# An induced-attention block and a rational mixture layer on one core: the odd unit's numerator ahead of the next mask, token sums from accumulated exponentials, and the second layer thirteen ticks behind with fifteen rooms

## The chip, the cores and the metric

The kernel runs on one core of a Trainium2 chip. The metric is the device time of one execution in microseconds (us). The engines are named as in the profile: PE (matmul; PEld are its weight loads), DVE (vector), ACT (scalar activation), POOL (GpSimd) and SP, which only issues DMAs. Each runs its own instructions in order and waits for the others by semaphores.

## The reference

There are 4 batches of 12480 tokens with 128 channels, and 32 inducing points. First the inducing points attend over the tokens, then the tokens attend over the 32 results. Each token then goes through two layers with 2048 hidden values, with a rational function between them:

```python
def mab(q, kv):
    s = scale * (q @ kv.transpose(0, 2, 1))
    s = s - s.max(-1, keepdims=True)
    a = np.exp(s)
    a /= a.sum(-1, keepdims=True) + 1e-09
    return a @ kv
h = mab(I, x)
attn_out = mab(x, h)
...
h = x @ w_in
h2 = h * h
h3 = h2 * h
P = a[0] + a[1] * h + a[2] * h2 + a[3] * h3
Q = 1.0 + np.abs(b[0]) * np.abs(h) + np.abs(b[1]) * h2
g = P / (Q + 1e-06)
return (g @ w_out).astype(np.float32)
```

## The kernel before

**Units and ticks.** A chunk is 480 tokens; a batch has 26 chunks. The hidden layer is cut into 8 parts of 256, so a chunk has 8 units and the whole run 832. One unit is a tile of 128 partitions x 2 x 480. `fast_ticks` (L777) writes out one loop over ticks t; in tick t it issues pieces of work for units of different age, and the order in which it issues them is the order on each engine (`InOrder`, L147, pins it; since all calls go through L157 there, the profile puts that line to nearly everything, and groups are told apart by their tiles).

**One unit's way.** `first` (L729) is the first layer into a PSUM tile `hp` (3 rooms). For an *even* unit DVE takes |h| into `u` (the **mask**, group `u<-hp`, L807); POOL makes the **opening** (|h| + k1, group `l<-u,all`, L813) into a tile of tag `l`; a tick later DVE makes the **even numerator** (`l<-hp,all,l`, L802), the last reader of `hp`. For an *odd* unit ACT takes **Abs** (`u<-hp,all`, L821) in its own tick, and DVE makes the **odd numerator** (`l<-u,all,hp`, L810) a tick later, also the last reader of `hp`. The two `u` of an even and an odd unit lie in one pair tile. ACT turns the pairs into the reciprocal of the denominator: four **Ln** (`u<-u`, L816) and four **Sigmoid** (`u<-u,all`, L818) in eight ticks, with a table load at each turn from one to the other. The variable `turn` (L788) counts the eight ticks. Exponentials of the attention go in at turn 4, ahead of the first Sigmoid.

In an odd tick the even unit that is 11 ticks old gets its last **product** on DVE (`l<-l,all,u`, L799: all operands in SBUF), and the odd unit that is 10 ticks old gets the same in two steps on POOL (`last_on_pool`, L827: `u<-l,all`, which writes into the `u` that the product reads, then `l<-u`). `second` (L744) multiplies the unit that is 12 ticks old with `w_out` into the PSUM tile `po` and adds up the 8 units of a chunk there. The `l` tile of a unit lives from its opening or numerator to this matmul; there are 14 rooms of `l`.

So DVE's order over a pair of ticks is: mask, odd numerator, other work, product, even numerator, other work. POOL's is: opening, `u<-l,all`, `l<-u`, with other work behind the opening or behind `l<-u`.

**The other work.** `side` (L680) closes each tick. It moves a finished `po` to SBUF by an **oT** copy on DVE and issues the store (`fetch`, L762), and then hands out steps of two generators as far as the spare time of each engine allows (`SPARE`, L175): `ahead` (L633) prepares the next batch (`pass1`: scores and their maxima; `pooled`: sums of tokens weighted by exponentials; `piece`, `linear`: the first layer's weights times the attention's result), and `attend` (L658) scores the tokens of the current batch a few chunks ahead. A unit with part 0 of its chunk is `late` (L790): its second layer is issued at the end of the tick, behind `side`.

**Token sums.** `pass1` leaves scores in the tile `e`; `exp_rows` (L380) exponentiates them in place. `pooled` (L403) turns them into tiles `eT` (2 rooms) and multiplies them with token rows, `x_rows` (L282), tiles of 4 x 129 columns, of which the last is filled with ones by POOL; so column 128 of the result is the sum of the exponentials. H, the normalised result, is turned and repeated into `HT` (2 rooms), which `piece`, `linear` and the scoring of the tokens read. `scored` is the last batch whose scoring is issued.

**The start.** `before` (L858) runs `pass1` and `pooled` for batch 0 and loads and converts the weights, with the first layer's PSUM rooms lent out; the raw weights lie in rooms of `l`.

## Time and profile before

| | us |
|---|---|
| median of 3 runs | 2594.55 |
| the runs | 2594.13 to 2599.68 |
| the profiled execution | 2594.75 |
| its span, from the first to the last instruction | 2592.9 |

The profile page gives the busy time of each engine, the chain of work that ended last, and groups of like instructions with count, busy time, mean duration and the idle time ahead of them with its releaser. In a group `out<-in`, names are those of tiles. The waits list how long an engine waited for which releaser; the timeline lists instructions of an engine in order of time, where a bracket gives the idle time ahead of one. The mean granted TensorE clock of the run was 0.966. The start takes about 115 us; the first oT copy is at 156.3 us, the last at 2587.7 us, and there are 104, one for each chunk. `pass1`, `pooled` and `piece` of later batches end at about 1700 us; after that `attend` alone runs beside the units.

### The profile page before, as it was taken

Reading aid. Unit: us, or ns where it says so; the run is one execution under the profiler, and the core shown is the slowest. Engines: PE = TensorE matmul, PEld = TensorE weight load, DVE = VectorE, ACT = ScalarE, POOL = GpSimd, SP = SyncE. Lnnn points to the kernel's source line nnn. Section 1 sums busy time; section 2 is a strip of 40 time slices with the busy share of each in tenths; the row PEclk is TensorE's granted clock in tenths of the full one; section 3 lists DMA queues with packets and bytes.
Section 4 is the critical chain, followed back from the end, with each engine's and each line's share of the span. In section 5 each row is a group of like instructions: output and inputs, shape, how many; then the busy total and the mean of one; then the engine's idle time right before and its main releaser. Section 6 shows DMA issues by size and latency. Waiting matters only on the chain.

```text
span 2592.9 us, 24006 instructions
## 1 busy us (share of the span) xinstructions
PE 2249.2 (87%) x7508; PEld 1233.8 (48%) x7508; DVE 2210.1 (85%) x2318; ACT 2244.9 (87%) x1590; POOL 2011.4 (78%) x1420
## 2 busy tenths in 40 slices
PE   7798888999899789989988898888888888888887
PEld 4544444555454355544544465444435434434333
DVE  6578778899899889899898888988889888888886
ACT  1488889989889999888899998899999999999996
POOL 2267767888787788888687887887888887888887
PEclk9699989999999999999999999999999999999999
DMA  7222201211222012112321131011101001000000
GB/s 251 73 62 78 73 27 52 71 50 31 70 83 80 19 31 76 50 48 63 92 55 48 35 88 38 16 42 31 46 27 50 27 20 38 20 22 24 17 17 17
DMA packets 117357, 133.68 MB, mean 52 GB/s; under 512 B 13544, under 2 KB 115816, under 8 KB 117224
## 3 DMA queue, kind: packets, MB, share of 16 engines
q1 hardware_dynamic: 117224, 132.06, 17.6%
q8 instruction: 64, 1.05, 0.2%
q14 instruction: 69, 0.57, 0.1%
HBM read 80.89 MB, written 25.56 MB: 41 GB/s over the span
## 4 chain that ended last, share of the span: by engine, by line
DVE 32%; PE 22%; ACT 19%; POOL 18%; issue 6%; DMA 1%; SPq 1%; DVEq 0%; POOLq 0%; ACTq 0%
DVE l L157 21%; ACT u L157 13%; POOL l L157 13%; PE po L157 13%; DVE u L157 7%; ACT L157 4%; POOL u L157 4%; PE hp L157 3%; PE ph L157 2%; PE pd L157 2%; DVE oT L157 1%; POOL a L157 1%; SPq L157 1%; DVE asm L157 1%; DMA x<-x_t 1%
## 5 line engine op out<-in xcount | busy, mean ns | idle before, releaser
L157 PE MATMUL po<-l,w_out 128*128 128x480 f32 x3328 | 1545.8, 592 | 188.4 <-POOL l L157 183.6
L157 PEld LDWEIGHTS po<-l,w_out 128*128 128x128 f32 x3328 | 607.3, 194 | 773.0 <-issue 419.7
L157 POOL TENSOR_TENSOR l<-u 128x960 f32<-128x960 f32 x416 | 932.2, 2241 | 34.7
L157 ACT ACTIVATE u<-u 128x1920 f32<-128x1920 f32 x416 | 739.8, 1799 | 193.2 <-DVE l L157 143.0
L157 PE MATMUL hp<-at,st 128*128 128x480 f32 x1664 | 742.7, 529 | 98.3 <-DVE l L157 91.1
L157 ACT ACTIVATE u<-u,all 128x1920 f32<-128x1920 f32 x416 | 766.1, 1887 | 1.2
L157 POOL TENSOR_SCALAR u<-l,all 128x960 f32<-128x960 f32 x416 | 445.5, 1071 | 392.8 <-DVE l L157 363.4
L157 DVE SCALAR_TENSOR_TENSOR l<-l,all,u 128x960 f32<-128x960 f32 x416 | 597.8, 1437 | 105.7 <-ACT u L157 105.3
L157 DVE SCALAR_TENSOR_TENSOR l<-hp,all,l 128x960 f32<-128x960 f32 x416 | 503.5, 1210 | 121.8 <-POOL l L157 114.0
L157 POOL TENSOR_SCALAR l<-u,all 128x960 f32<-128x960 f32 x416 | 555.6, 1336 | 64.7 <-DVE u L157 63.7
L157 DVE TENSOR_SCALAR u<-hp 128x960 int32<-128x960 int32 x416 | 477.0, 1147 | 75.6 <-PE hp L157 74.3
L157 PEld LDWEIGHTS hp<-at,st 128*128 128x128 f32 x1664 | 312.6, 193 | 431.3 <-issue 325.3
L157 DVE SCALAR_TENSOR_TENSOR l<-u,all,hp 128x960 f32<-128x960 f32 x416 | 500.3, 1203 | 0.3 <-ACT u L157 0.3
L157 ACT ACTIVATE u<-hp,all 128x960 f32<-128x960 f32 x416 | 434.7, 1045 | 36.4 <-PE hp L157 36.3
L157 ACT ACT_TABLE_LOAD x234 | 300.2, 1283 | 4.9 <-PEq L942 0.7
L157 PE MATMUL ph<-x,eT 120*32 120x129 f32 x832 | 105.8, 280 | 9.0 <-DMA x<-x_t 6.3
L157 PEld LDWEIGHTS pd<-HT,xTb 128*120 128x120 f32 x832 | 103.3, 198 | 9.7 <-DMA xTb<-x_c 4.3
L157 PE MATMUL pd<-HT,xTb 128*120 128x32 f32 x832 | 100.5, 277 | 5.2 <-DMA xTb<-x_c 4.1
L157 PEld LDWEIGHTS ph<-x,eT 120*32 120x32 f32 x832 | 88.9, 112 | 28.0 <-issue 21.5
L157 DVE COPY oT<-po 128x480 f32<-128x480 f32 x104 | 67.3, 647 | 21.6 <-PE po L157 21.3
L157 PE MATMUL po<-at,st 128*128 128x480 f32 x104 | 80.7, 776 | 0.0
L157 PE MATMUL pc<-xTa,ind 128*128 128x480 f32 x156 | 72.2, 566 | 1.9 <-DMA xTa<-x_c 1.9
(84 smaller groups left out, 621.6 us busy)
## 6 DMA issues: line engine op xcount, KB each, us to landing
x<-x_t SPq DMA_DIRECT2D x104, 240.0 KB, 3.5
xTb<-x_c SPq DMA_DIRECT2D x104, 240.0 KB, 2.8
at<-hl SPq DMA_DIRECT2D x416, 60.0 KB, 2.0
out<-oT SPq DMA_DIRECT2D x104, 240.0 KB, 2.0
xTa<-x_c SPq DMA_DIRECT2D x78, 240.0 KB, 2.8
xTw<-x_c SPq DMA_DIRECT2D x5, 960.0 KB, 10.3
raw<-w_in SPq DMA_DIRECT2D x4, 480.0 KB, 14.2
raw<-w_out SPq DMA_DIRECT2D x5, 384.0 KB, 5.9
```

Of the source, the lines that this page charges most:

```text
L157: ins = call(*args, **kw)
```

## The change

- **Order on DVE.** In an even tick the odd numerator of the unit before is issued ahead of the mask.
- **Second layer.** `second` takes the unit that is 13 ticks old, `late` goes by that unit, the loop has one tick more, and `l` has 15 rooms. A late unit now falls in an odd tick, and the oT copy in an even one.
- **Token sums.** The exponentials' activation adds up its results by row (`accum_out`) into a tile `sums`; at the end DVE reduces it to one column and a matmul with `sum4` (four stacked unit matrices) adds the four row groups. The column of ones, its memsets on POOL and the 129th column of the sums are gone; a token-row tile is now contiguous.
- **Memory.** `eT` has one room (in the start it takes rooms of `l`), `HT` has one room, and its matmul waits until the batch before is scored; the table of constants has 88 columns.

```diff
@@ -47,7 +47,7 @@
 
     def __init__(self, nc, pool, moe_a, moe_b):
         self.nc, self.pool, self.n = nc, pool, 0
-        self.all = pool.tile([P, 128], F32, name="all")
+        self.all = pool.tile([P, 88], F32, name="all")
         ab = pool.tile([P, 6], F32, name="ab")
         nc.sync.dma_start(out=ab[:, 0:4], in_=moe_a.rearrange("(o n) -> o n", o=1).broadcast_to((P, 4)))
         nc.sync.dma_start(out=ab[:, 4:6], in_=moe_b.rearrange("(o n) -> o n", o=1).broadcast_to((P, 2)))
...
@@ -259,6 +259,10 @@
         self.ident4 = cp.tile([M, 4, M], F32, name="ident4")
         for j in range(4):
             nc.vector.tensor_copy(out=self.ident4[:, j], in_=self.ident[0:M, 0:M])
+        self.sum4 = cp.tile([P, M], F32, name="sum4")
+        nc.vector.tensor_copy(out=self.sum4, in_=self.ident[:, 0:M])
+        for j in range(1, 4):
+            nc.vector.tensor_tensor(out=self.sum4, in0=self.sum4, in1=self.ident[:, M * j:M * j + M], op=ALU.add)
         self.w_in = cp.tile([C, self.F], F32, name="w_in")
         self.w_out = cp.tile([P, self.NF, C], F32, name="w_out")
 
...
@@ -273,22 +277,21 @@
             dst = self.w_out[:, c].rearrange("p f d -> p (f d)")
             parts.append((self.w_out_d[P * c.start:P * c.stop, :].rearrange("(f p) d -> p f d", p=P), dst, C * (c.stop - c.start)))
         for n, (src, dst, width) in enumerate(parts):
-            tag, bufs = ("l", 14) if width > 2 * P else ("oT", 2)
+            tag, bufs = ("l", 15) if width > 2 * P else ("oT", 2)
             raw = self.mp.tile([P, width], mybir.dt.int64, tag=tag, name=f"raw{n}", bufs=bufs)
             self.nc.sync.dma_start(out=raw if len(src.shape) == 2 else raw.rearrange("p (f d) -> p f d", d=C), in_=src)
             yield raw, dst, width
 
 
     def x_rows(self, b, n):
-        t = self.ap.tile([TP, HB, C + 1], F32, tag="xa", name=f"x{b}_{n}", bufs=4)
-        self.nc.sync.dma_start(out=t[:, :, 0:C], in_=self.x_t[b, :, HB * n:HB * n + HB, :])
-        self.nc.gpsimd.memset(t[:, :, C:], 1.0)
+        t = self.ap.tile([TP, HB, C], F32, tag="xa", name=f"x{b}_{n}", bufs=4)
+        self.nc.sync.dma_start(out=t, in_=self.x_t[b, :, HB * n:HB * n + HB, :])
         self.issued["x", b, n] = self.tick
         return t
 
     def x_columns(self, b, n, kind):
         if kind == "a":
-            t = self.ap.tile([C, HB * (C + 1)], F32, tag="xa", name=f"xTa{b}_{n}", bufs=4)[:, 0:BT]
+            t = self.ap.tile([C, HB * C], F32, tag="xa", name=f"xTa{b}_{n}", bufs=4)[:, 0:BT]
         else:
             t = self.ap.tile([C, BT], F32, tag="xTb", name=f"xTb{b}_{n}", bufs=4)
         self.nc.sync.dma_start(out=t, in_=self.x_c[b, :, BT * n:BT * n + BT])
...
@@ -338,6 +341,8 @@
         e = ap.tile([P, self.NG, BT], F32, tag="e", name=f"e{b}")
         mxs = ap.tile([P, self.NG, 2], F32, tag="mxs", name=f"mxs{b}")
         nc.gpsimd.memset(mxs, -3.0e38)
+        self.sums[b] = ap.tile([P, self.NG], F32, tag="sums", name=f"sums{b}")
+        nc.gpsimd.memset(self.sums[b], 0.0)
         xs = self.wide_columns(b) if self.boot else self.cols.pop((b, "a"))
         for g in range(self.NG):
             nb = min(4, self.NB - 4 * g)
...
@@ -384,7 +389,7 @@
         rows = slice(0, M * min(4, self.NB - 4 * (g + n - 1)))
         if n == 2 and rows.stop < P:
             n, rows = 1, slice(0, P)
-        self.nc.scalar.activation(e[rows, g:g + n], e[rows, g:g + n], AF.Exp, bias=nmc[rows], scale=1.0 / math.sqrt(C))
+        self.nc.scalar.activation(e[rows, g:g + n], e[rows, g:g + n], AF.Exp, bias=nmc[rows], scale=1.0 / math.sqrt(C), accum_out=self.sums[b][rows, g:g + 1])
         self.e_done[b] = g + n
         if g + n < self.NG:
             if self.boot:
...
@@ -404,7 +409,7 @@
 
         nc, ap = self.nc, self.ap
         e = self.e[b]
-        acc = ap.tile([M, C + 1], F32, tag="acc", name=f"acc{b}")
+        acc = ap.tile([M, C], F32, tag="acc", name=f"acc{b}")
         xs = self.xs.pop(b)
 
         def turned(g):
...
@@ -414,7 +419,10 @@
                 if c == 0:
                     pt = self.misc(f"pt{b}_{g}").rearrange("p (c n) -> p c n", c=HB)
                 nc.tensor.transpose(out=pt[0:TP, c, rows], in_=e[rows, g, TP * c:TP * c + TP], identity=self.ident[rows, rows])
-            eT = ap.tile([TP, HB, P], F32, tag="eT", name=f"eT{b}_{g}", bufs=2)
+            if self.boot:
+                eT = self.mp.tile([TP, 2, BT], F32, tag="l", name=f"eT{b}_{g}", bufs=15).rearrange("p a n -> p (a n)")[:, 0:HB * P].rearrange("p (c n) -> p c n", n=P)
+            else:
+                eT = ap.tile([TP, HB, P], F32, tag="eT", name=f"eT{b}_{g}")
             yield from self.act(lambda: nc.scalar.activation(eT[:, :, rows], pt[0:TP, :, rows], AF.Identity, bias=0.0, scale=1.0))
             eTs.append(eT)
 
...
@@ -438,27 +446,34 @@
                     ph = self.misc(f"ph{b}_{g}")
                 if c == 0 and 0 < 4 * g + j < self.NB - 3:
                     xs.append(self.x_rows(b, 4 * g + j + 3))
-                nc.tensor.matmul(ph[0:M, 0:C + 1], eT[:, c, M * j:M * j + M], xs[4 * g + j][:, c, :], start=(k == 0), stop=(k == HB * nb - 1))
+                nc.tensor.matmul(ph[0:M, 0:C], eT[:, c, M * j:M * j + M], xs[4 * g + j][:, c, :], start=(k == 0), stop=(k == HB * nb - 1))
             yield "v", 0.2
             if g == 0:
-                nc.vector.tensor_copy(out=acc, in_=ph[0:M, 0:C + 1])
+                nc.vector.tensor_copy(out=acc, in_=ph[0:M, 0:C])
             else:
-                nc.vector.tensor_tensor(out=acc, in0=ph[0:M, 0:C + 1], in1=acc, op=ALU.add)
+                nc.vector.tensor_tensor(out=acc, in0=ph[0:M, 0:C], in1=acc, op=ALU.add)
             self.free()
+        yield "v", 0.1
+        es = ap.tile([P, 1], F32, tag="es", name=f"es{b}")
+        nc.vector.tensor_reduce(out=es, in_=self.sums[b], axis=mybir.AxisListType.X, op=ALU.add)
+        yield "pe", 0.2
+        pr = self.misc(f"prs{b}")
+        nc.tensor.matmul(pr[0:M, 0:1], self.sum4, es, start=True, stop=True)
         yield "v", 0.2
         rs = ap.tile([M, 1], F32, tag="rs", name=f"rs{b}")
-        nc.vector.tensor_scalar(out=rs, in0=acc[:, C:], scalar1=1e-9, scalar2=None, op0=ALU.add)
+        nc.vector.tensor_scalar(out=rs, in0=pr[0:M, 0:1], scalar1=1e-9, scalar2=None, op0=ALU.add)
+        self.free()
         nc.vector.reciprocal(out=rs, in_=rs)
         yield "v", 0.2
         H = ap.tile([M, C], F32, tag="H", name=f"H{b}")
-        nc.vector.tensor_scalar(out=H, in0=acc[:, 0:C], scalar1=rs, scalar2=None, op0=ALU.mult)
+        nc.vector.tensor_scalar(out=H, in0=acc, scalar1=rs, scalar2=None, op0=ALU.mult)
+        while own is None and b > 1 and self.scored < b - 1:
+            yield "wait", 0
         yield "pe", 0.3
         pt = self.misc(f"HT{b}")
         nc.tensor.matmul(pt[:, 0:4 * M], H, self.ident4.rearrange("p a m -> p (a m)"), start=True, stop=True)
         yield "v", 0.2
-        while own is None and self.scored < b - 2:
-            yield "wait", 0
-        HT = own if own is not None else ap.tile([C, 4 * M], F32, tag="HT", name=f"HT{b}", bufs=2)
+        HT = own if own is not None else ap.tile([C, 4 * M], F32, tag="HT", name=f"HT{b}")
         nc.vector.tensor_copy(out=HT, in_=pt[:, 0:4 * M])
         self.free()
         self.HT[b] = HT
...
@@ -783,15 +798,16 @@
         n = len(units)
         at = lambda t: units[t] if 0 <= t < n else None
         self.first(units[0])
-        for t in range(n + 13):
+        for t in range(n + 14):
             u, last, d = at(t), at(t - 1), at(t - 11)
             group, turn = divmod(t - 6, 8)
             w = at(8 * group + 2 * (turn % 4))
-            late = at(t - 12) and at(t - 12).key[2] == 0
+            done = at(t - 13)
+            late = done and done.key[2] == 0
             if late:
                 self.fetched = self.fetch()
-            if at(t - 12) and not late:
-                self.second(at(t - 12))
+            if done and not late:
+                self.second(done)
             if at(t + 1):
                 self.first(at(t + 1))
             if t % 2:
...
@@ -801,15 +817,15 @@
                 if last:
                     V.scalar_tensor_tensor(out=last.g, in0=last.h, scalar=p.k2, in1=last.g, op0=ALU.add, op1=ALU.mult)
             else:
+                if last:
+                    last.g = self.new(last, "l", 15)
+                    V.scalar_tensor_tensor(out=last.g, in0=last.u, scalar=p.k1, in1=last.h, op0=ALU.add, op1=ALU.mult)
                 if u:
                     u.pair = self.mp.tile([P, 2, 2, BT], F32, tag="u", name=f"u{u.i}", bufs=7)
                     u.u = u.pair[:, 0]
                     V.tensor_scalar(out=u.u.bitcast(I32), in0=u.h.bitcast(I32), scalar1=0x7FFFFFFF, scalar2=None, op0=ALU.bitwise_and)
-                if last:
-                    last.g = self.new(last, "l", 14)
-                    V.scalar_tensor_tensor(out=last.g, in0=last.u, scalar=p.k1, in1=last.h, op0=ALU.add, op1=ALU.mult)
                 if u:
-                    u.g = self.new(u, "l", 14)
+                    u.g = self.new(u, "l", 15)
                     G.tensor_scalar(out=u.g, in0=u.u, scalar1=1.0, scalar2=p.k1, op0=ALU.mult, op1=ALU.add)
             self.run_act(turn == 4)
             if w and turn < 4:
...
@@ -821,7 +837,7 @@
                 A.activation(u.u, u.h, AF.Abs, bias=p.back, scale=1.0)
             self.side(u or units[-1])
             if late:
-                self.second(at(t - 12))
+                self.second(done)
         self.fetch()
 
     def last_on_pool(self, d, before):
...
@@ -858,7 +874,7 @@
     def before(self):
 
         nc = self.nc
-        self.e, self.xs, self.HT, self.issued, self.tick = {}, {}, {}, {}, 0
+        self.e, self.xs, self.HT, self.issued, self.sums, self.tick = {}, {}, {}, {}, {}, 0
         self.boot, self.direct, self.holder, self.who = True, True, None, None
         self.exps, self.exp_q, self.e_done = [], [], {}
         nc.scalar.preload_act_table_set("natural_log_exp_and_others")
```

More of the change, by code (lines that the diff above doesn't have):

```diff
@@ L837, in general_ticks @@
             self.first(u)
-            d, y, g, h = self.new(u, "u", 7), self.new(u, "l", 14), self.new(u, "l", 14), u.h
+            d, y, g, h = self.new(u, "u", 7), self.new(u, "l", 15), self.new(u, "l", 15), u.h
             r = self.ps_h.tile([P, 2, 512], F32, tag="hp", name=f"r{u.i}")[:, :, 0:BT]
```

## The prediction

> **What bounds the kernel now.** I read the page first, then the groups and the waits, then the timeline of each engine in a quiet stretch, and last the chain of the start.
>
> ```profile
> span 2592.9 us, 24006 instructions
> PE 2249.2 (87%) x7508; PEld 1233.8 (48%) x7508; DVE 2210.1 (85%) x2318; ACT 2244.9 (87%) x1590; POOL 2011.4 (78%) x1420
> DVE 32%; PE 22%; ACT 19%; POOL 18%; issue 6%; DMA 1%; SPq 1%; DVEq 0%; POOLq 0%; ACTq 0%
> ```
>
> Four engines are busy for 78 to 87% and the chain walks over all four: no engine is full, a loop between them sets the pace. I look for that loop where attention no longer disturbs it, late in the run. Columns: start, duration, engine, operation.
>
> ```profile
> 2307.88 0.64 DVE L157 COPY oT<-po 128x480 f32<-128x480 f32 x1
> ...
> 2310.63 1.75 DVE L157 SCALAR_TENSOR_TENSOR l<-l,all,u 128x960 f32<-128x960 f32 x1
> ...
> 2315.62 1.34 DVE L157 SCALAR_TENSOR_TENSOR l<-l,all,u 128x960 f32<-128x960 f32 x1
> 2317.93 1.22 DVE L157 SCALAR_TENSOR_TENSOR l<-hp,all,l 128x960 f32<-128x960 f32 x1 [0.97 <-POOL l L157]
> 2319.06 1.15 DVE L157 TENSOR_SCALAR u<-hp 128x960 int32<-128x960 int32 x1
> 2320.13 1.21 DVE L157 SCALAR_TENSOR_TENSOR l<-u,all,hp 128x960 f32<-128x960 f32 x1
> 2321.25 1.21 DVE L157 SCALAR_TENSOR_TENSOR l<-l,all,u 128x960 f32<-128x960 f32 x1
> 2323.35 1.22 DVE L157 SCALAR_TENSOR_TENSOR l<-hp,all,l 128x960 f32<-128x960 f32 x1 [0.89 <-POOL l L157]
> ...
> 2327.43 1.30 DVE L157 SCALAR_TENSOR_TENSOR l<-l,all,u 128x960 f32<-128x960 f32 x1 [0.67 <-ACT u L157]
> ...
> 2329.78 0.64 DVE L157 COPY oT<-po 128x480 f32<-128x480 f32 x1
> ```
>
> ```profile
> 2310.30 1.07 POOL L157 TENSOR_SCALAR l<-u,all 128x960 f32<-128x960 f32 x1
> ...
> 2315.93 1.97 POOL L157 TENSOR_SCALAR l<-u,all 128x960 f32<-128x960 f32 x1
> 2317.88 1.07 POOL L157 TENSOR_SCALAR u<-l,all 128x960 f32<-128x960 f32 x1
> 2319.03 2.24 POOL L157 TENSOR_TENSOR l<-u 128x960 f32<-128x960 f32 x1
> 2321.25 2.07 POOL L157 TENSOR_SCALAR l<-u,all 128x960 f32<-128x960 f32 x1
> 2323.30 1.06 POOL L157 TENSOR_SCALAR u<-l,all 128x960 f32<-128x960 f32 x1
> ```
>
> From one oT copy to the next are 21.90 us for eight ticks, 5.475 a pair of ticks. The product on DVE (l<-l,all,u) and the ops of POOL never run side by side. Where the product is first (2321.25, done 2322.46), POOL's opening (l<-u,all) takes 2.07 instead of 1.07 and ends 0.86 after it, and the even numerator (l<-hp,all,l), which needs the opening, waits 0.89. Where the opening is first (2310.30, done 2311.37), the product takes 1.75 and ends 1.01 after it. One of the two prices is paid unless something stands between. POOL's own three ops (start to start 1.15, 2.22, about 1.07) and a product of its own turn fill the pair too.
>
> I measured every step from one even numerator to the next in DVE's timeline, 403 of them; the first and the last:
>
> ```profile
> 160.73 1.21 DVE L157 SCALAR_TENSOR_TENSOR l<-hp,all,l 128x960 f32<-128x960 f32 x1
> ...
> 2547.87 1.21 DVE L157 SCALAR_TENSOR_TENSOR l<-hp,all,l 128x960 f32<-128x960 f32 x1
> ```
>
> They average 5.92 us. 226 of them have neither a wait for PE or ACT nor an attention op on POOL: 83 without other DVE work average 5.54, 108 with up to 1.1 us of it 5.56, 35 with more 5.92, all 5.61. So other DVE work up to 1.1 us is free today. 116 with a wait for PE or ACT average 6.28, which is 116 x 0.67 = 78 us of loss. 62 with an attention op on POOL average 6.39; the change leaves these ops alone.
>
> **The change part by part.** *Numerator ahead of the mask.* From the rows: even numerator to the next op 1.13, mask to the next 1.07, odd numerator to the next 1.12, product to the even numerator 2.10 when POOL is pushed back. Their sum, 5.42, has the same terms in both orders. What changes is where the opening can start. Now it may start under the odd numerator; with the mask last, the product follows on DVE at once, while POOL hears of the mask's end only then, so the product is always first, unless DVE has other work between mask and product. Work before the numerator is then no longer covered: it delays mask, opening and the next even numerator by its full length. Work after the mask stays free up to about 0.95, but costs about 0.13, since POOL's next op (u<-l,all) must then wait for the product. By the same timeline a step has 0.16 us of other work before the mask and 0.16 after the numerator, and the oT copy's 0.14 (0.57 in every fourth), which goes from the first place to the second with the later tick. New step: 5.42 + 0.16 + 0.47 x 0.13 (the share with work after the mask) + 0.02 for what exceeds 0.95 = 5.66 against 5.61: 403 x 0.05 = **+20 us**. Ends: all other work after the mask gives 5.48, -52 us; all of it ahead of the numerator gives 5.76, +60 us. I take the middle, as the places are half and half today.
>
> Against that stand the waits (total, times, longest).
>
> ```profile
> PE po L157 <- POOL l L157: 183.6, 175, 2.7
> ACT u L157 <- DVE l L157: 143.0, 89, 3.8
> DVE l L157 <- POOL l L157: 114.0, 115, 2.0
> DVE l L157 <- ACT u L157: 105.6, 78, 3.6
> ...
> DVE u L157 <- PE hp L157: 74.3, 59, 5.6
> ...
> DVE l L157 <- POOL x L157: 7.6, 8, 1.0
> ```
>
> ```profile
> 2318.41 1.79 ACT L157 ACTIVATE u<-u 128x1920 f32<-128x1920 f32 x1
> 2321.43 1.80 ACT L157 ACTIVATE u<-u 128x1920 f32<-128x1920 f32 x1 [1.23 <-DVE l L157]
> 2323.14 1.05 ACT L157 ACTIVATE u<-hp,all 128x960 f32<-128x960 f32 x1
> 2324.20 1.28 ACT L157 ACT_TABLE_LOAD   x1
> 2325.50 3.68 ACT L157 ACTIVATE u<-u,all 128x1920 f32<-128x1920 f32 x2
> ```
>
> Once in eight ticks the fourth Ln waits for the odd numerator (ends 2321.34), and the product two steps on waits for the first Sigmoid: 2327.43 - 2321.34 = 6.09 us by way of ACT, against 5.42 by way of DVE. With the numerator first, DVE's way becomes 1.12 + 1.07 + 5.42 - 1.21 = 6.40, and the wait is gone. It stays where an exponential is put in ahead of that Sigmoid with a table load of its own:
>
> ```profile
> L157 ACT ACT_TABLE_LOAD x234 | 300.2, 1283 | 4.9 <-PEq L942 0.7
> ```
>
> 234 loads less 2 x 104 leaves 26 such groups. There about 2.1 us come on top; of the 1.8 that DVE waits, 0.9 is the lock's price saved: 26 x 0.9 = 23 us, and about 0.5 each for the odd numerator that then waits for Abs, 13 us. That new wait is the one this order adds: behind the numerator stand mask, opening and product, and all slip with it. Over the rows like 2323.14 Abs ends after the even numerator (an oT copy taken off) in 87 of 406 odd ticks, 34.8 us in all; that is the new wait's upper end, zero the lower.
>
> *Second layer a tick later.* PE stands 183.6 us in second-layer matmuls until POOL's product is there; a tick more (2.96 us, half of 5.92) covers nearly all, as the longest is 2.7. Little of that is on the path late in the run, but early it makes PE late with hp, and the mask waits 74.3 us for it. The numerator first also frees its hp room 1.07 earlier and asks for the next hp 1.12 later. I leave 12 of the 74.3 on the path (ends 0 and 50). What is late next is the opening behind the mask. The room of l is still free two ticks ahead of its writer, as now, and the tick more at the end brings no work with it. So of 78 us 23 + 13 + 12 = 48 stay: **-30 us** (ends -78 and +35).
>
> *Token sums.* 104 memsets leave POOL; DVE waited 7.6 us for them: **-5** (0 to -8). Added are some DVE ops below 0.3 and one small matmul a batch, and the accumulator on 16 exponentials, which no row prices (0 to 0.2 each, the lower end being the likelier for one sum in a 1 us op): under 4 us, mostly in free places. In the start:
>
> ```profile
> 42.68 4.35 DMA x<-x_t
> ...
> 49.87 4.04 DMA x<-x_t
> ...
> 69.06 3.54 DMA x<-x_t
> ```
>
> ```profile
> x<-x_t SPq DMA_DIRECT2D x104, 240.0 KB, 3.5
> xTb<-x_c SPq DMA_DIRECT2D x104, 240.0 KB, 2.8
> ```
>
> The x tile lands whole, as xTb does, 0.7 us sooner; three such stretches and the waits on POOL memsets between: **-6** (0 to -12).
>
> *Memory.*
>
> ```profile
> 1579.52 0.41 DVE L157 TENSOR_REDUCE amx<-pd 120x8 f32<-120x256 f32 x1
> ...
> 1626.32 0.27 DVE L157 COPY HT<-HT 128x128 f32<-128x128 f32 x1
> ```
>
> One eT room: the next transposes come behind the matmuls that read it. One HT room: the last HT is written 47 us after the last scores that read the one before it, so the new wait finds nothing to wait for; were that cover gone, the fourth batch's units begin only some 390 us later. Cost 0. The xa and l rooms change size and number, not order; the queue of SP issues the same DMAs.
>
> **Sum.** +20 - 30 - 5 - 6 = -21 us. On 2594.75 (span and 1.85 around it, 0.2 above the median 2594.55): **2574**.
>
> **The rivals.** *Waits gone:* all 78 us, with a little more other work behind the mask, so that the step without waits stays 5.61: 2594.75 - 78 - 5 - 6 = **2506**. For it: PE's 183.6 us are the largest wait of a matmul; against: 5.42 is a floor in this order, and late in the run the step is 5.475 already. *Uncovered work:* attention's DVE ops come ahead of the numerator, where nothing hides them (+60), and the waits for PE only move from the mask to Abs and the numerator (0 in place of -30): 2594.75 + 60 - 11 = **2644**. For it: half of these ops stand at that place today. It decides from the point where they exceed 0.21 us a step there: 403 x 0.05 more eats the 21 us. *Cancelled:* the PE waits were slack, the terms meet at zero: **2595**.
>
> *Lock in full:* an opening that began only at the product's end would end 1.07 behind it, not 0.86; over the 214 steps (0.53 x 403) without work after the mask, 0.21 each, that is +45 us, **2619**. The two rows above speak for 0.86 to 0.94, so I give it little. The Trainium skill, "SBUF — State Buffer", section "A bandwidth-pool intuition that's wrong (but worth ruling out)", has the loser of the shared port "blocked until DVE-end + ~115 ns"; by its figure the sum would be an estimated 2644.
>
> **How the numbers follow.** Forecast 0.38 (2555 to 2589), waits gone 0.17, cancelled 0.12, uncovered work 0.28, lock in full 0.05. Below 0.2% (5.2 us) a measurement of this kernel can't be told from no change. Faster 0.38 + 0.17 = 0.55, same 0.12, slower 0.33. The range reaches to 2510 and 2645, near the prices of the outer rivals, with about 0.1 beyond each.
>
> **What would show it.** Right: POOL l gone as releaser of PE po; ACT u as releaser of l<-l,all,u near 47 us; the wait of l<-hp,all,l for POOL above 114; openings of 2.07 in most quiet steps; a late period of 21.7. Wrong: the numerator waiting for ACT over 40 us, quiet steps above 5.6, or openings of 1.07, by which POOL would have been first after all.

## The result, and the profile after

The changed kernel takes 2630.16 us (median of 4 runs, 2622.96 to 2630.49) against 2596.02 for the one before on the same chip (4 runs): the ratio is 1.0123, with an interval of 1.0102 to 1.0144. It is slower by 34 us. The profiled execution took 2630.03 us.

The page of the changed kernel: span, busy times, the chain that ended last by engine, and three groups of instructions (busy time, mean ns of one, idle time before them and its releaser).

```profile
span 2628.0 us, 23717 instructions
...
PE 2301.5 (88%) x7516; PEld 1267.8 (48%) x7516; DVE 2224.1 (85%) x2326; ACT 2253.2 (86%) x1606; POOL 2091.1 (80%) x1320
...
DVE 36%; POOL 25%; PE 17%; issue 10%; ACT 9%; DMA 1%; SPq 1%; DVEq 0%; POOLq 0%; ACTq 0%
...
L157 PE MATMUL po<-l,w_out 128*128 128x480 f32 x3328 | 1577.0, 605 | 57.9 <-DVE oT L157 50.3
...
L157 POOL TENSOR_SCALAR l<-u,all 128x960 f32<-128x960 f32 x416 | 644.0, 1548 | 169.4 <-DVE u L157 161.2
...
L157 DVE SCALAR_TENSOR_TENSOR l<-hp,all,l 128x960 f32<-128x960 f32 x416 | 504.4, 1212 | 234.1 <-POOL l L157 234.1
```

The opening's row before the change:

```profile
L157 POOL TENSOR_SCALAR l<-u,all 128x960 f32<-128x960 f32 x416 | 555.6, 1336 | 64.7 <-DVE u L157 63.7
```

Before, the chain went over DVE, PE, ACT and POOL for 32, 22, 19 and 18%. Now DVE and POOL alone hold 61% of it, and ACT has fallen to 9%. The opening, 1336 ns before, has a mean of 1548, and the even numerator waits twice as long for it.

The waits of the changed kernel (total, times, longest):

```profile
DVE l L157 <- POOL l L157: 234.1, 233, 2.3
...
PE hp L157 <- DVE l L157: 188.0, 200, 3.2
POOL l L157 <- DVE u L157: 161.2, 262, 10.5
...
ACT u L157 <- DVE l L157: 130.3, 84, 6.6
ACT u L157 <- PE hp L157: 106.9, 72, 6.1
...
DVE l L157 <- ACT u L157: 68.9, 54, 4.1
PE po L157 <- DVE oT L157: 50.3, 59, 0.9
...
DVE u L157 <- PE hp L157: 9.1, 8, 3.5
...
PE po L157 <- POOL l L157: 6.2, 4, 2.7
```

and one wait of the kernel before:

```profile
PE hp L157 <- DVE l L157: 91.1, 77, 3.6
```

PE hardly waits for POOL's product any more (6.2 us, 183.6 before), nor the mask for PE (74.3 before). What grew is what stands on the loop of DVE and POOL: the opening waiting for the mask (63.7 before), the even numerator waiting for the opening (114.0). PE's time of waiting has not gone but changed its place: 188.0 us for a room of hp (91.1 before).

A quiet stretch, DVE's timeline (start, duration, engine, operation, idle before and releaser):

```profile
2309.29 1.21 DVE L157 SCALAR_TENSOR_TENSOR l<-l,all,u 128x960 f32<-128x960 f32 x1
2311.47 1.22 DVE L157 SCALAR_TENSOR_TENSOR l<-hp,all,l 128x960 f32<-128x960 f32 x1 [0.97 <-POOL l L157]
2312.60 1.20 DVE L157 SCALAR_TENSOR_TENSOR l<-u,all,hp 128x960 f32<-128x960 f32 x1
2313.73 1.15 DVE L157 TENSOR_SCALAR u<-hp 128x960 int32<-128x960 int32 x1
2314.79 1.21 DVE L157 SCALAR_TENSOR_TENSOR l<-l,all,u 128x960 f32<-128x960 f32 x1
2316.97 1.22 DVE L157 SCALAR_TENSOR_TENSOR l<-hp,all,l 128x960 f32<-128x960 f32 x1 [0.97 <-POOL l L157]
...
2320.29 0.65 DVE L157 COPY oT<-po 128x480 f32<-128x480 f32 x1
2320.86 1.69 DVE L157 SCALAR_TENSOR_TENSOR l<-l,all,u 128x960 f32<-128x960 f32 x1
2322.47 1.21 DVE L157 SCALAR_TENSOR_TENSOR l<-hp,all,l 128x960 f32<-128x960 f32 x1
```

And POOL's timeline there:

```profile
2309.48 1.96 POOL L157 TENSOR_SCALAR l<-u,all 128x960 f32<-128x960 f32 x1 [0.18 <-DVE u L157]
...
2320.48 1.06 POOL L157 TENSOR_SCALAR l<-u,all 128x960 f32<-128x960 f32 x1 [0.17 <-DVE u L157]
```

From even numerator to even numerator are 5.50 us. The product starts 0.19 us before the opening and is done at 2310.50; the opening ends at 2311.44, 0.94 behind it. In this stretch the opening is first only where the oT copy stands between mask and product: it then takes 1.06, and the even numerator doesn't wait. Over the whole run product and opening run into each other in 359 of 411 steps; the product starts first in 207 of them, against 80 of 341 before (counted in both timelines). From oT copy to oT copy, chunks 72 to 96 take 22.97 us each on average (551.2 / 24), 22.42 before (538.0 / 24).

### The profile page after: what moved, and what is told of

Same layout as the page of the kernel before. It is cut to its first block, busy times and chain, and to the rows that moved or that the text cites. A ratio compares the mean times of both kernels' runs of the same rounds, so it can differ in the third digit from the quotient of the medians.

```text
span 2628.0 us, 23717 instructions
## 1 busy us (share of the span) xinstructions
PE 2301.5 (88%) x7516; PEld 1267.8 (48%) x7516; DVE 2224.1 (85%) x2326; ACT 2253.2 (86%) x1606; POOL 2091.1 (80%) x1320
## 4 chain that ended last, share of the span: by engine, by line
DVE 36%; POOL 25%; PE 17%; issue 10%; ACT 9%; DMA 1%; SPq 1%; DVEq 0%; POOLq 0%; ACTq 0%
DVE l L157 21%; POOL l L157 20%; PE po L157 10%; DVE u L157 9%; ACT u L157 6%; POOL u L157 3%; PE ph L157 2%; ACT L157 2%; PE hp L157 2%; DVE oT L157 2%; PE pd L157 2%; DVE asm L157 1%; POOL a L157 1%; SPq L157 1%; DMA x<-x_t 1%
## 5 line engine op out<-in xcount | busy, mean ns | idle before, releaser
L157 PE MATMUL po<-l,w_out 128*128 128x480 f32 x3328 | 1577.0, 605 | 57.9 <-DVE oT L157 50.3
L157 PEld LDWEIGHTS po<-l,w_out 128*128 128x128 f32 x3328 | 650.7, 202 | 609.7 <-issue 483.1
L157 PE MATMUL hp<-at,st 128*128 128x480 f32 x1664 | 722.6, 518 | 193.4 <-DVE l L157 188.0
L157 POOL TENSOR_SCALAR l<-u,all 128x960 f32<-128x960 f32 x416 | 644.0, 1548 | 169.4 <-DVE u L157 161.2
L157 DVE SCALAR_TENSOR_TENSOR l<-hp,all,l 128x960 f32<-128x960 f32 x416 | 504.4, 1212 | 234.1 <-POOL l L157 234.1
L157 DVE SCALAR_TENSOR_TENSOR l<-l,all,u 128x960 f32<-128x960 f32 x416 | 590.3, 1419 | 49.9 <-ACT u L157 49.8
L157 PEld LDWEIGHTS hp<-at,st 128*128 128x128 f32 x1664 | 303.5, 194 | 571.5 <-issue 337.6
L157 DVE SCALAR_TENSOR_TENSOR l<-u,all,hp 128x960 f32<-128x960 f32 x416 | 499.2, 1200 | 19.3 <-ACT u L157 19.1
L157 PE MATMUL ph<-x,eT 120*32 120x128 f32 x832 | 106.0, 282 | 15.2 <-DMA x<-x_t 13.2
```

Of the source, the lines that this page charges most:

```text
L157: ins = call(*args, **kw)
```

## The experiments

Twelve kernels were run. Ratios are against the kernel before on the same chip, with their 95% interval.

| label | kernel | us | ratio |
|---|---|---|---|
| e1_mask_first | change with the mask first again | 2620.36 | 1.0116 (1.0094 to 1.0138) |
| e2_lag12 | change with twelve ticks again | 2660.41 | 1.0273 (1.0256 to 1.0290) |
| e3_sums_only | both undone: token sums and memory alone | 2613.57 | 1.0084 (1.0062 to 1.0105) |
| e4_first_once | change, numerator first at turn 2 alone | 2590.49 | 0.9999 (0.9981 to 1.0018) |
| e5_sums_folded | e3 with the new steps in one | 2592.96 | 1.0018 (1.0003 to 1.0034) |
| e6_idle_tick | before plus one empty tick | 2612.39 | 1.0081 (1.0061 to 1.0101) |
| e7_folded_first | e5 plus numerator first | 2643.63 | 1.0208 (1.0186 to 1.0230) |
| e8_lag13_plan | e5 plus thirteen ticks, old list of ticks nearly kept | 2639.63 | 1.0191 (1.0170 to 1.0212) |
| e9_once_only | before plus numerator first at turn 2 | 2577.16 | 0.9924 (0.9905 to 0.9944) |
| e10_oT_behind_mask | e7 with the oT copy behind the mask | 2717.45 | 1.0474 (1.0439 to 1.0509) |
| e11_psum_first | e7 with the product's second factor in hp | 2449.90 | 0.9442 (0.9423 to 0.9462) |
| e12_psum_mask | the same with the mask first | 2508.75 | 0.9667 (0.9638 to 0.9696) |

### Which of the parts costs: e1, e2 and e3

e1 puts the odd numerator back behind the mask, and e2 puts the second layer back by a tick; e3 does both.

```diff
# e2 (and e3)
-        for t in range(n + 14):
+        for t in range(n + 13):
...
-            done = at(t - 13)
+            done = at(t - 12)
```

> The changed kernel with the old order on DVE (mask, then the odd numerator); second layer thirteen ticks behind, fifteen rooms and the new token sums stay. Lock theory (the numerator ahead of the mask makes the opening always come behind the product): the loss sits in the order alone, so this is below the kernel before: 2545 to 2585 us, with openings of about 1.3 us mean and the even numerator's wait for POOL back near 114 us. Second-layer theory (the later tick, with the oT copy in an even tick and the late unit in an odd one, costs): 2615 to 2635 us, as the changed kernel.

> The changed kernel with the second layer twelve ticks behind again; the numerator stays ahead of the mask. Lock theory: slower than the kernel before, 2620 to 2660 us, since the order stays and PE's waits for POOL come back. Second-layer theory: 2580 to 2600 us.

> The changed kernel with both the old order on DVE and the second layer twelve ticks behind: what is left is the token sums from the activation's accumulator, the single rooms of eT and HT and the fifteenth room. Lock and second-layer theory both: 2583 to 2597 us, at most some 11 us below the kernel before. A third theory, that sums or memory cost: above 2605 us.

With twelve ticks the order costs 47 us (2613.57 to 2660.41). With thirteen it costs 10 by the times (2620.36 to 2630.16); but the kernel before took 2596.02 us beside the changed kernel and 2591.26 beside e1 to e4, and by the ratios it is 2, which the intervals don't tell from nothing. In the same way the change is 30 us faster than e2 by the times and 39 by the ratios: that is what thirteen ticks gain with the numerator first, together with the other places that attention's steps then get. With the mask first they gain nothing (+7, e1 against e3). And the part that was to save 11 us, e3, loses some 20 with neither of the others in it. So neither theory holds alone: e1 lies where the second-layer theory had it, e2 at the upper end of the lock theory's range, and e3 where the third theory had it.

The row of PE's second-layer matmuls in e3's page, with twelve ticks, and PE's wait for a room of hp:

```profile
L157 PE MATMUL po<-l,w_out 128*128 128x480 f32 x3328 | 1546.2, 592 | 174.3 <-POOL l L157 171.0
...
PE hp L157 <- DVE l L157: 113.9, 88, 3.7
```

and in e1, with thirteen:

```profile
L157 PE MATMUL po<-l,w_out 128*128 128x480 f32 x3328 | 1547.4, 595 | 4.6 <-POOL l L157 3.7
...
PE hp L157 <- DVE l L157: 252.8, 220, 4.1
```

The tick takes 167 us of waits for POOL off PE, and the time does not fall: PE now waits 139 us more for rooms of hp. With the mask first most of this waiting only changed its place.

### Why the token sums cost: e5 and e6

The planner starts an attention step only if its declared cost fits into what the tick has left. The change adds steps (a reduction, a matmul, and their `yield`s). e5 issues the same instructions within the steps that were there:

```diff
-        yield "v", 0.1
+        yield "v", 0.2
         es = ap.tile([P, 1], F32, tag="es", name=f"es{b}")
...
-        yield "pe", 0.2
         pr = self.misc(f"prs{b}")
...
-        yield "v", 0.2
         rs = ap.tile([M, 1], F32, tag="rs", name=f"rs{b}")
```

e6 leaves the kernel before as it is and lets the token sums of batch 1 pass one tick without work:

```diff
+        for _ in range(1 if not self.boot and b == 1 else 0):
+            yield "wait", 0
```

> The kernel with the old order and twelve ticks (token sums and memory alone, 2613.6 us) once more, but the reduction, the small matmul and the reciprocal of the sums are issued in one step of the generator ahead, so that this step list has the same ticks as in the kernel before: its pass1 and pooled of batches 1, 2 and 3 end at ticks 147, 238, 328, 412 and 504, as before, instead of 149, 251, 333, 429 and 523. Plan theory (the new steps cost nothing by themselves, but shift the ticks at which all later attention work is placed): 2583 to 2597 us. Operation theory (accumulator, single rooms or token-row loads cost): 2606 to 2620 us.

> The kernel before with one empty step (a wait of a tick) in pooled of batch 1 and nothing else. Its list of ticks then is nearly that of the token sums alone (149, 251, 331, 429, 521). Plan theory: 2605 to 2618 us. Operation theory: 2588 to 2598 us, as the kernel before.

e5 is 2 us from the kernel before (5 by its ratio); e6, which computes exactly what that does, is 21 us slower. So the token sums' instructions cost next to nothing; what costs is the tick at which everything behind them in attention then falls. The oT copies of chunks 40 and 48 in DVE's timeline show the place, in e5:

```profile
1137.90 0.64 DVE L157 COPY oT<-po 128x480 f32<-128x480 f32 x1
...
1330.33 0.65 DVE L157 COPY oT<-po 128x480 f32<-128x480 f32 x1
```

in e6:

```profile
1146.53 0.64 DVE L157 COPY oT<-po 128x480 f32<-128x480 f32 x1
...
1347.09 0.65 DVE L157 COPY oT<-po 128x480 f32<-128x480 f32 x1
```

and in the changed kernel:

```profile
1132.08 0.65 DVE L157 COPY oT<-po 128x480 f32<-128x480 f32 x1
...
1338.05 0.66 DVE L157 COPY oT<-po 128x480 f32<-128x480 f32 x1 [0.57 <-PE po L157]
```

These eight chunks take 192.4 us in e5, 200.6 in e6 and 206.0 in the changed kernel. Late in the run, from chunk 72 to chunk 96, where little attention work is left, e5 and e6 take the same 538 us again, so the loss lies where more of attention's instructions are placed. That some 20 us of the changed kernel's loss are of this kind is inferred from e3, e5 and e6, all with twelve ticks. With thirteen only a part of it can be seen: the same eight chunks take 204.1 us in e1 and 205.0 in e4 (below), with the new steps, and 192.2 in e8 (below), whose list of ticks is nearly the old one. The whole amount was not shown there, as e8 loses elsewhere.

### What the order costs and what it does: e7, e9 and e4

e7 is e5 with the odd numerator ahead of the mask, so neither the list of ticks nor the distance stands between the two.

```diff
             else:
+                if last:
+                    last.g = self.new(last, "l", 15)
+                    V.scalar_tensor_tensor(out=last.g, in0=last.u, scalar=p.k1, in1=last.h, op0=ALU.add, op1=ALU.mult)
                 if u:
...
-                if last:
-                    last.g = self.new(last, "l", 15)
-                    V.scalar_tensor_tensor(out=last.g, in0=last.u, scalar=p.k1, in1=last.h, op0=ALU.add, op1=ALU.mult)
```

> The first kernel of this call with the numerator ahead of the mask, everything else as there, so that the order is changed on the old list of ticks and with twelve ticks. Lock theory: 40 to 55 us above that kernel, as between the two kernels with twelve ticks of the call before (2660.4 and 2613.6 us), thus 2625 to 2645 us if the plan theory holds. A theory by which the order's price is itself a matter of the list of ticks: less than 20 us above.

With twelve ticks the order alone costs 51 us (2592.96 to 2643.63). The rows of its page, opening and even numerator:

```profile
L157 POOL TENSOR_SCALAR l<-u,all 128x960 f32<-128x960 f32 x416 | 712.0, 1711 | 214.4 <-DVE u L157 201.8
...
L157 DVE SCALAR_TENSOR_TENSOR l<-hp,all,l 128x960 f32<-128x960 f32 x416 | 505.5, 1215 | 308.1 <-POOL l L157 308.1
```

and of e5's, with the mask first:

```profile
L157 POOL TENSOR_SCALAR l<-u,all 128x960 f32<-128x960 f32 x416 | 554.2, 1332 | 65.8 <-DVE u L157 63.0
...
L157 DVE SCALAR_TENSOR_TENSOR l<-hp,all,l 128x960 f32<-128x960 f32 x416 | 503.5, 1210 | 120.7 <-POOL l L157 120.4
```

The even numerator waits 308.1 us for the opening; in e5 it is 120.4. e9 puts the numerator first only at turn 2, where the fourth Ln waits for it, and on the kernel before; e4 does the same to the changed kernel.

```diff
# e9, on the kernel before
             else:
+                if last and (turn == 2):
+                    last.g = self.new(last, "l", 14)
+                    V.scalar_tensor_tensor(out=last.g, in0=last.u, scalar=p.k1, in1=last.h, op0=ALU.add, op1=ALU.mult)
...
-                if last:
+                if last and not (turn == 2):
```

> The kernel before, with the numerator ahead of the mask in one of four pairs of ticks only (turn 2, where the fourth Ln waits for it); twelve ticks, fourteen rooms, old token sums, old list of ticks. Lock theory: the order pays only where a Ln waits for the numerator; the waits of ACT u for DVE l (143 us) and of DVE l for ACT u (105.6 us) fall by half or more, one pair in four pays the lock: 2555 to 2580 us. If the order only ever costs: above 2597 us. If the once-only order needs the later second layer to be worth anything: 2585 to 2597 us.

> The changed kernel with the numerator ahead of the mask in one of four pairs of ticks only, at turn 2, where the fourth Ln waits for it; the mask comes first in the other three. Lock theory: three of four pairs are free of the order's price and the wait of Ln and Sigmoid still goes: 2535 to 2580 us, at or below the kernel with the mask always first. Second-layer theory: 2610 to 2630 us.

e9 takes 0.9924 of the time before: it is the version that beats both kernels, by 19 us the one before and by some 50 the change. The waits of e9 (before: 143.0 and 105.6 us):

```profile
ACT u L157 <- DVE l L157: 118.0, 76, 5.6
...
DVE l L157 <- ACT u L157: 47.7, 34, 3.2
```

The second of the two waits fell by more than half, as expected, the first only by a sixth. So the gain by way of ACT, on which the prediction counted, is real, and one turn in four has it. On the other three together the same edit costs more than it gains. e4 against e1 says so with thirteen ticks: 2620.36 to 2590.49, where the order at all four turns gives 2630.16. e4 itself came out 10 us above its expected range, and by the ratios 19 above e9, which has the same order with twelve ticks and the old list of ticks.

### Whether the lock makes the order's price: e11 and e12

The product of DVE reads two operands in SBUF. e11 takes the second from hp, which lies in PSUM, so the even units' values are no longer the reference's; the instructions and what they wait for stay. e12 does so with the mask first.

```diff
-                    V.scalar_tensor_tensor(out=d.g, in0=d.g, scalar=p.k3, in1=d.u, op0=ALU.add, op1=ALU.mult)
+                    if last:
+                        V.scalar_tensor_tensor(out=d.g, in0=d.g, scalar=d.u[:, 0, 0:1], in1=last.h, op0=ALU.add, op1=ALU.mult)
+                    else:
+                        V.scalar_tensor_tensor(out=d.g, in0=d.g, scalar=p.k3, in1=d.u, op0=ALU.add, op1=ALU.mult)
```

> Numerator first, old list of ticks, twelve ticks, and the product of even units takes its second factor from the tile hp in PSUM instead of the reciprocal in SBUF (the reciprocal is still read as a column of scalars, so the waits stay); the even units' values are therefore not the reference's. Lock theory (an op of DVE with two operands in SBUF and an op of POOL never run side by side): openings are all near 1.07 us, the quiet step falls from 5.50 to 5.15 to 5.3 us, where ACT is full, and the whole to 2400 to 2530 us. If the long openings come from anything else (their own start, the queue of POOL): 2630 to 2650 us with openings near 2 us.

> As the run above, with the mask first; the even units' values are again not the reference's. Lock theory: without the lock the order is worth little, so this is within 25 us of the run above, on either side, instead of 50 us below it; 2400 to 2530 us. If the order costs by something other than the lock: 40 to 55 us below the run above.

The opening and the product in e11's page:

```profile
L157 POOL TENSOR_SCALAR l<-u,all 128x960 f32<-128x960 f32 x416 | 445.9, 1072 | 240.3 <-DVE u L157 221.5
...
L157 DVE SCALAR_TENSOR_TENSOR l<-l,u,hp 128x960 f32<-128x960 f32 x411 | 494.4, 1203 | 87.0 <-ACT u L157 86.7
```

Both have their own length again, 1.07 and 1.20 us, whichever starts first, and the time falls by 194 us in e11 and by 84 in e12, each against its own pair (e7, e5; by the ratios, as the pairs ran on another chip, 199 and 91). Above all the order's sign turns: with the lock the numerator first costs 51 us, without it it gains 59 (2508.75 to 2449.90), where the lock theory had expected at most 25 either way. So the reordering is sound in itself, and its price is who comes first. Product and opening run into each other in most steps in either order. With the mask first (e5) the opening starts first in 263 steps, and the product then takes 0.27 us longer on average; the product starts first in 77. With the numerator first (e7) the product starts first in 274 steps, and the opening, for which the even numerator waits, then takes 0.89 us longer. The Trainium skill, "SBUF — State Buffer", section "Who interferes with whom", says that a DVE instruction with two SBUF inputs contends with a GpSimd instruction that reads SBUF, and one with at most one SBUF input, outside the 2-port modes, does not. These runs agree (openings of 1711 ns on average in e7 and 1072 in e11).

### Two runs that missed: e8 and e10

e8 asks what thirteen ticks are worth alone, with the token sums folded, the mask first, and the oT copy's cost charged at the tick where it was charged before, so that the list of ticks is nearly the old one.

```diff
-        if self.fetch() or self.fetched:
+        self.fetch()
+        if self.due:
...
+            self.due = at(t - 12) and at(t - 12).key[2] == self.NP - 1
```

> Old order, thirteen ticks, fifteen rooms, folded sums, and the planner charges the oT copy's 0.56 us of DVE time in the tick in which it did with twelve ticks; pass1 and pooled then end at 147, 238, 327, 409 and 496. Lag theory (a tick more frees PE of its waits for POOL and that is worth time): 2560 to 2582 us. If a tick more is worth nothing by itself: 2583 to 2600 us. If the later tick costs on its own: above 2603 us.

It came out at 1.0191. Most of its loss sits in two groups of eight chunks, 32 to 40 (208.9 us against 190.9 before) and 48 to 56 (214.3 against 189.0), and its waits point to a cause that is neither theory's:

```profile
PE ph L157 <- DMA x<-x_t: 36.2, 9, 7.9
...
DVE acc L157 <- PE ph L157: 31.1, 7, 6.8
```

The x tiles of batches 2 and 3 come late. Of the 36.2 us, 14.4 lie in the first of the two groups and 5.9 in the second, so for the second this is a part at most. In the quiet chunks from 72 to 96, where nothing of this reaches, e8 takes 537.1 us and e5 538.3: there the later second layer gains a microsecond. e1 takes 547.2 us for the same chunks, with e8's order and distance but other ticks for attention's steps. For the whole run e8 tells nothing.

e10 asks whether work on DVE is free again where it stands between mask and product: in e7, where it is ahead of the numerator, the oT copy is held back until behind the next mask.

```diff
-        if self.fetch() or self.fetched:
+        if self.full:
+            self.held, self.full = self.full, None
...
+                if self.held:
+                    self.full, self.held = self.held, None
+                    self.fetch()
```

> The kernel with the numerator first on the old list of ticks and with twelve ticks (2643.6 us), with the oT copy alone moved from the end of its odd tick to the place right behind the next mask. Cover theory (with the numerator first, DVE work ahead of it delays the opening by its full length and work behind the mask is free, and that is what the later second layer gained by moving the oT copy): 103 x 0.57 = 59 us at most, so 2585 to 2612 us. PE theory (the later second layer gained by freeing PE of its waits for POOL, which stay here): 2632 to 2650 us.

At 2717.45 us it is the slowest of all. There is one room for po, and a copy that is held back holds PE. In PE's timeline:

```profile
2339.23 1.07 PE L157 MATMUL po<-l,w_out 128*128 128x480 f32 x2 [1.99 <-DVE oT L157]
```

and in its waits:

```profile
ACT u L157 <- PE hp L157: 219.8, 113, 6.1
PE po L157 <- DVE oT L157: 163.6, 92, 2.9
...
DVE u L157 <- PE hp L157: 141.7, 101, 4.5
```

PE stands 163.6 us for the copy, and mask and Abs for PE. As a test of the cover the run is inconclusive, as it adds a wait larger than what it asks about. Only the steps without a wait for PE or ACT and without attention on POOL speak to it: with 0.1 to 1.1 us of other DVE work they average 5.67 in e10 and about 5.9 with the copy ahead of the numerator.

## Why the prediction was wrong, and where it was right

**The loop** was read rightly. Product and opening exclude each other; with the numerator first the product comes first unless other work stands between it and the mask (207 steps, 80 before); the opening that comes second takes 1.96 (2.07 was foreseen), POOL l is nearly gone as releaser of PE po (6.2 us), the even numerator's wait for POOL grew (234.1, above 114), the product's wait for ACT's u fell (68.9, of which 49.8 are the product's own; 47 was foreseen). But one of the signs of being wrong came, a quiet step above 5.6 (5.76), and the late period is 22.97 instead of 21.7.

**The new step** is the term that failed, +20 us. In the steps without a wait for PE or ACT and without attention on POOL, measured in DVE's timeline as before the change, the mean is 5.76 in 278 steps: 131 without other work 5.55, 101 with up to 1.1 us 5.66, 46 with more 6.56. The kernel before had 5.61, and 5.66 was foreseen. Over 403 steps that is 403 x 0.15 = +60 us in place of +20. Two sizes in its sum were wrong:

- The floor, 5.42. It took 2.10 from product to even numerator from a row where opening and product were issued at the same moment (2321.25). In the new order the opening starts on the mask's signal, 0.19 behind the product, and ends 0.94 after it, not 0.86: 2311.47 - 2309.29 = 2.18. The floor is 5.50, 0.08 more, 403 x 0.08 = 32 us. This goes a part of the way of the rival "lock in full", for which the prediction had the two rows and chose the lower.
- The work ahead of the numerator, taken as 0.16 a step. Counted at every step of the changed kernel's DVE timeline, 0.206 us of other work a step stand between even and odd numerator, and 0.293 behind the mask, the oT copy (101 of 101) among the latter as foreseen. That is 403 x 0.046 = 19 us more. The rival "uncovered work" was to decide from 0.21, and there it stands.

Together they turn the foreseen 5.66 into 5.79, 0.03 above what was measured. Against the kernel before, though, the floor costs nothing: steps without other work took 5.54 there and take 5.55 now, so with 5.42 the forecast had counted on a gain that did not come. Nearly all of the 0.15 is uncovered work. The steps with more than 1.1 us of other work show it best: 5.92 before, 6.56 now, which is 0.11 of the 0.15 (46 of 278 steps), where the prediction had 0.02 for what exceeds the cover; those with less, 5.56 and 5.66, give the other 0.04. The prediction had said that work ahead of the numerator is paid in full, and then took the middle of its ends because "the places are half and half today".

**The waits**, -30. All steps together went from a mean of 5.92 to 6.02, +40 us; less the +60 above, the steps with waits and attention give -20, in which the cost of the shifted list of ticks (below) is contained. So the size was about right, as far as a remainder can say. Of its reasons, the way by ACT holds: e9 has it alone and gains 19 us. The odd numerator's new wait for ACT came to 19.1 us. What the mask's shorter wait for PE is worth was not shown: e1 has 167 us fewer of PE's waits for POOL and no gain, but its mask still waits 62.2 us for PE (81.9 in e3). What the later tick gains with the numerator first, 30 to 39 us (e2 to the change), seems to be of another kind: the oT copy falls behind the mask, where it is covered. In steps without those waits, 0.1 to 1.1 us of other work take the step to 5.93 in e2 (115 steps) and to 5.66 in the change (101), more work to 6.90 (37) and 6.56 (46). The prediction had that in its new step, as the oT copy's 0.14.

**Token sums and start**, -5 and -6. The instructions cost next to nothing, as said (e5); each of the 16 exponentials now has a read of the accumulator behind it, of 0.19 us, near the upper end of what was allowed. The first oT copy, which comes a tick later now, starts at 155.8 us against 156.3. But e6, which starts as the kernel before does, has it at 153.4, and e5 and e3, with twelve ticks and nearly the same start, at 151.3 and 159.0: the start's 6 us can't be told from this spread. x lands 0.2 us sooner (3.3 us, 3.5 before), not 0.7. What the prediction did not have at all is the list of ticks. It put the added steps "mostly in free places" and left the schedule as it was; e3, e5 and e6 show +20 us for that alone, with no instruction to blame.

**Memory**, 0: nothing in the waits of the changed kernel names the single eT or HT room among its larger entries, and e5, which has the memory change, equals the kernel before.

**The sum by kernels.** From 2594: the list of ticks +20 (e3, e6), the order +50 (e7), the later tick with this order -30 to -39 (e2 to the change), which gives 2625 to 2634 against 2630 measured. With the later tick taken ahead of the order it is +20, +7 (e1 over e3) and +2 to +10 (the change over e1). The terms depend on each other, and each path ends at the changed kernel by the way it is put together, so this is a balance, not a proof. In particular, undoing the order alone in the changed kernel (e1) does not bring back the time of before. The time lies between the rivals "lock in full", 2619, and "uncovered work", 2644. The mechanism of the second is in it, but so is the list of ticks, which no rival had; that the sum falls near them is luck.

## What to carry to other kernels

Before an op is moved on a full engine, count for every other op of that engine on which side of it it will stand: work that was free beside a wait is paid in full ahead of the op which that wait hangs on. Where two engines exclude each other on some ops, move an op only at the turns at which something waits for it; here, with twelve ticks, one turn in four gained 19 us and all four lost 51. And in a kernel whose side work is placed by a planner, an edit changes every later placement: compare it with a kernel that only shifts the placement (here one empty tick, 21 us) before its time is put down to its instructions.

## What the runs showed of the hardware

- **The lock's tail is short.** The opening, 1.07 us by itself, ends 0.86 to 0.94 after a product with two SBUF operands that began first (rows at 2321.25 before and 2309.48 after the change), less than its own length. The Trainium skill's "blocked until DVE-end + ~115 ns" ("SBUF — State Buffer", section "A bandwidth-pool intuition that's wrong (but worth ruling out)"; the page measured it on a DMA's descriptors) would have it end 1.19 after, an estimate from its figure and the 1.07; the trace disagrees, so part of the opening seems to be done while the product still runs, which was not tested. For this product, an operand in PSUM ends the exclusion altogether (e11, e12: 1072 and 1073 ns for 416 openings each).
- **PE's clock was lower with thirteen ticks.** The granted clock of the profiled executions of the kernel before and of the changed one:

```profile
core 0: 2592.9 us, clock 0.966
```

```profile
core 0: 2628.0 us, clock 0.939
```

All kernels with thirteen ticks lie low (e1 0.944, e4 0.950, e8 0.943), those with twelve high (e3 0.968, e7 0.968, e9 0.971, e2 0.971), except e10 (0.934, where PE stands for its copies). The cause was not tested. Longer single waits of PE don't show: those for POOL ahead of po had a mean of 1.05 us before (183.6 in 175), those for DVE ahead of hp have 0.94 in the changed kernel (188.0 in 200). The clock does not decide the time: e4 runs at 0.950 and is as fast as the kernel before.
